# Batch 1's attention outputs with queries on partitions, turned by TensorE, and placed ahead of chunk 24

## The chip, the cores and the metric

The kernel runs on one core of one Trainium2 chip. The metric is the device time of one execution in microseconds (us). Seven executions of the kernel before took 259.46 to 267.28 us, with a median of 260.74 us; the profiled one is the one that took 259.46 us.

## What is computed

The reference is a windowed attention with sink tokens, followed by a gated feed-forward network (ReGLU). It has 4 batches, 8 heads, 768 positions and a head dimension of 64; the network has d_model = 512 and d_ff = 1536.

```
scores = (q @ k.T) / sqrt(64)
keep   = (key < 4) | ((0 <= query - key) & (query - key < 128))
a      = softmax(where(keep, scores, -1e9))
x      = (a @ v), heads side by side: 3072 tokens x 512
out    = (relu(x @ w_gate) * (x @ w_val)) @ w_out
```

The inputs are float32. The kernel computes with bfloat16 operands and float32 sums.

## The kernel before, in words

**Units.** Two heads of one batch make a unit; there are four units to a batch and sixteen in all, `U[4b + p]`. Their 64 head dimensions each fill the 128 partitions.

**Attention of a unit.** `load_kq` or `load_half` brings q and k, a cast on GpSimd makes them bfloat16, and they are turned so that the head dimension lies on partitions. Batch 0 is turned in halves (`T_half`, L292), batch 1 in whole units (`T`, L277), both by TensorE through PSUM; batches 2 and 3 go through DRAM with a transposing DMA (`turn`). ScalarE and VectorE copy the turned keys and queries to `KQ`, where a second copy of the keys at odd offsets is made (`odd_tiles`, L199). `Sg(u, s)` (L316) computes one of three groups of scores, keys on partitions and queries along the free dimension, takes the exponential on ScalarE (L330) and multiplies with a mask on VectorE (L337).

**Outputs of a unit.** There are two ways. `V(u, part)` (L372) multiplies a half of the queries with a block of ones for the sums and with v for the outputs; these come out with the head dimension on partitions, as `xT` needs it, and VectorE turns, inverts and multiplies the sums (L359 to L369). The other way is `W(u)` (L384): queries on partitions, v and a column of ones side by side, so that the sums come with the outputs, then a reciprocal and one multiplication on VectorE. Its result `xn` still has to be turned; the kernel before does this with DMAs through DRAM (`x_to_dram`, `x_turn`). The kernel before takes `V` for batches 0 and 1 and `W` for batches 2 and 3.

**Feed-forward.** `chunk(b, g, m)` (L401) makes one block of 128 hidden columns for half a batch (384 tokens): four matmuls with `wg` (L408), Relu on ScalarE to `gs` (L411), four matmuls with `wv` (L413), and their product on VectorE to `hT` (L415). `ffn2(b, t, m)` (L419 on; matmul L428) adds one of twelve parts of the output of 128 tokens; after the twelfth, ScalarE copies the sum to `ot` (L432) and SP stores it.

**Order.** It is written out by hand, and every engine follows the order in which its instructions are issued. After a head with the first half of batch 0, there are 96 slots, one for each chunk: slot s has chunk s, so that chunk 24 is the first of batch 1. `prep[s]` holds what is issued ahead of the chunk (loads, casts, DMAs), `plan[s]` what follows it: T and H are turns, S scores, V and W outputs, with the unit and the group or half in digits ("S14" is group 4 of unit 1 of the batch). From slot 24 on, three `ffn2` matmuls close each slot; what is left of them at the end makes a tail. Chunk 24 needs the `xT` of all units of batch 1, for the first half of their queries, and chunk 36 for the second.

**Queues and buffers.** Loads and stores are issued by SP in program order, and weights by GpSimd (`load_w`, `load_wo`), which also does the casts of k, q and v in its own order. `gate(u)` (L151) is a small ScalarE copy into a load's buffer; the load waits for it, so it starts no earlier than ScalarE comes to that place. There are three k and q buffers, so unit 7's load needs the buffer that unit 4's cast has read. PSUM has four single banks `G` and two double ones `PP`. Chunks rotate through G[0] to G[2]; G[3] is for `ffn2` and the half turns; scores, outputs and whole turns take the next double bank (`pair`, L261). `wo` comes in three transfers of 512 KB, each for four of the twelve m.

Of the kernel before, what the change touches and what calls it, by code (L numbers as in the profile page):

```python
# [19 lines left out]
def kernel(  # L20
# [12 lines left out]
    nc = tc.nc  # L33
# [60 lines left out]
           5: (0, 0, 499, [(0, 0, 0, 247), (ODD, 120, 247, 499)])}  # L94

    VLAST = [(4, 2, 0, 252, 112), (6, 2, 252, 272, 364), (5, 2, 272, 416, 240), (4, 2, 416, 419, 364)]
    VSEG = [[(0, 0, 8, 252, 0), (1, 0, 252, 504, 120), (0, 0, 504, 507, 244), (2, 1, 0, 140, 244), (3, 1, 252, 264, 372)],
            [(2, 1, 140, 252, 0), (3, 1, 264, 504, 0), (2, 1, 504, 507, 112)] + VLAST]
    VSEG0 = [[(0, 0, 0, 247, 0), (1, 0, 247, 499, 120), (2, 1, 0, 140, 244), (3, 1, 140, 152, 372)],
             [(2, 1, 152, 267, 0), (3, 1, 267, 507, 0)] + VLAST]  # L100


    QSEG = [[(0, 0, 0)], [(0, 0, 128), (1, 0, 252)], [(1, 0, 376), (2, 1, 0), (0, 0, 504)],
# [47 lines left out]
    def gate(u):  # L151

        nc.scalar.copy(kf[u.i % NQ][0:1, 0:2], warm[0:1, :])
# [45 lines left out]
    def odd_tiles(u, copy):  # L199
        e = kE[u.i % NT]  # L200
        copy(odd(e)[:, :, 4:128], e[:, 120:876].rearrange("d (i c) -> d i c", c=252)[:, :, 0:124])
        sinks(u, copy)
# [62 lines left out]
    def two():  # L265
        if head[0]:
            srot[0] += 2
            return G[srot[0] % 4][:], G[(srot[0] + 1) % 4][:]
        x = pair()
        return x[:, 0, :], x[:, 1, :]  # L270
# [5 lines left out]

    def T(u):  # L277
        t = u.i % NT
        tk, tq = two()
        for x, ps in ((kn[u.i % 2], tk), (qn[u.i % 2], tq)):  # L280
            for n in range(NR):
                for h in range(2):
                    r = slice(64 * h, 64 * h + 64)
                    nc.tensor.transpose(ps.bitcast(BF16)[r, 64 * n:64 * n + 64], x[r, 64 * n:64 * n + 64], ident[r, r])  # L284
        vk, vq = (ps.bitcast(BF16)[:, 0:S].rearrange("d (n p) -> d p n", p=PR) for ps in (tk, tq))
        e = kE[t]
        to = lambda ap: ap.rearrange("d (p n) -> d p n", n=NR)
        nc.scalar.copy(to(e[:, 0:S]), vk)
        nc.vector.tensor_copy(to(qT[t]), vq)
        odd_tiles(u, nc.scalar.copy)  # L290

    def T_half(c):  # L292
        t, x = c % NP, c // NP
# [45 lines left out]
    ready = {}  # L339

    def sums(u, part, out, w):
        segs = (VSEG if u.b else VSEG0)[part]
        for i, (j, g, c0, c1, o0) in enumerate(segs):
            for h in range(2):
                nc.tensor.matmul(out=out[64 * h:64 * h + 64, o0:o0 + c1 - c0], lhsT=w(j, h),  # L345
                                 rhs=ee[u.i % NE][:, g, h, c0:c1], start=i == 0, stop=i == len(segs) - 1,
                                 skip_group_check=True)
# [36 lines left out]
    def W(u):  # L384

        ps = pair()
        for h in range(2):
            for t, segs in enumerate(QSEG):
                for i, (j, g, c0) in enumerate(segs):
                    nc.tensor.matmul(out=ps[:, h, 65 * t:65 * t + 65], lhsT=ee[u.i % NE][:, g, h, c0:c0 + 128],  # L390
                                     rhs=vn[u.b % 2][:, j, 2 * u.p + h, 0:65], start=t == 0 and i == 0,
                                     stop=t == 6 and i == len(segs) - 1, skip_group_check=True)
        o = ps[:, :, 0:455].rearrange("p h (t e) -> p h t e", e=65)
        x, r = xn[u.i % 2], rn[u.i % 2]
        nc.vector.reciprocal(r[:], o[:, :, :, 64])
        nc.vector.tensor_tensor(x[:].rearrange("p t (h d) -> p h t d", h=2), o[:, :, :, 0:64],  # L396
                                r[:].unsqueeze(3).to_broadcast([128, 2, 7, 64]), op=Alu.mult)

    gvn = [0]

# [21 lines left out]
    def ffn2(b, t, m):  # L422
        if m == 0:
            ops = OP[tail[0]]
            opn[0] += 1
            opend[b, t] = ops[opn[0] % len(ops)]
        op = opend[b, t]
        nc.tensor.matmul(out=op, lhsT=hT[b % 2][:, m, t * 128:(t + 1) * 128], rhs=wo[:, m, :],  # L428
                         start=m == 0, stop=m == FM - 1)
        if m == FM - 1:  # L430
            ot = outpool.tile([128, d_model], F32, name="ot")
            nc.scalar.copy(ot[:], op)  # L432
            nc.sync.dma_start(out=out[b * S + t * 128:b * S + (t + 1) * 128, :], in_=ot[:])

    with tc.manual_schedule():
# [65 lines left out]
        def put(s, y, n):  # L501
            st = (y[0], n * NP + int(y[1]), int(y[2]) if len(y) > 2 else 0)
            at[st] = s
            plan[s].append(st)

        for s, w in {0: "S04 S02 H1", 1: "S14 S12", 2: "H2", 3: "S24 S22 H3", 4: "S34 S32", 5: "V01", 6: "V11",
                     7: "V21", 8: "V31"}.items():
            for y in w.split():
                put(s, y, 0)
        for s, w in {12: "T0", 13: "T1", 14: "S00 S01", 15: "S10 S11", 16: "T2", 17: "S20 S21", 18: "V00",  # L510
                     19: "V10 T3", 20: "V20", 21: "S30 S31", 22: "V30 S02"}.items():
            for y in w.split():
                put(s, y, 1)
        for s, w in {24: "V01 S12", 26: "V11 S22", 28: "V21 S32", 30: "V31"}.items():
            for y in w.split():
                put(s, y, 1)
        for b, sl in ((2, {29: "S00 S01", 31: "S02 S10", 33: "S11 S12", 35: "S20 S21", 36: "W0", 37: "S22 S30",
# [3 lines left out]
            for s, w in sl.items():  # L521
                for y in w.split():
                    put(s, y, b)
        prep = [[] for _ in slots]
        prep[1] += [("half", 6), ("half", 7), ("v", 0, 3), ("v", 0, 4), ("w", 6, 8), ("v", 0, 5), ("v", 0, 6),
                    ("w", 8, 10), ("w", 10, 12)]
        prep[9] += [("setup3",), ("load", 4), ("load", 5), ("load", 6), ("lv", 1)]
        prep[10] += [("kq", 4), ("load", 7), ("kq", 5)]
        prep[13] += [("kq", 6)]
        prep[15] += [("v", 1, j) for j in range(7)]  # L530
        prep[8] += [("setup2", 0)]
        prep[16] += [("kq", 7), ("wo",)]
        for i, ts in ((8, (14, 18, 19, 23)), (9, (15, 20, 21, 25)), (10, (17, 21, 22, 27)), (11, (19, 22, 23, 29)),
                      (12, (30, 33, 35, 37)), (13, (32, 35, 37, 39)), (14, (34, 37, 39, 41)), (15, (36, 39, 41, 46))):
            for t, what in zip(ts, ("rows", "castrows", "td", "turn")):
# [12 lines left out]
        for s, (b, g, m) in enumerate(slots):  # L548
            for x in prep[s]:
                if x[0] == "kq":  # L550
                    cast_kq(U[x[1]])
                elif x[0] == "load":
                    gate(U[x[1]])
                    load_kq(U[x[1]])
                elif x[0] == "half":
                    cast_half(x[1])
                elif x[0] == "w":
                    load_w(*x[1:])
                elif x[0] == "wo":
                    for c in range(3):  # L560
                        load_wo(c)
                elif x[0] == "rows":
                    load_rows(U[x[1]])
                elif x[0] == "castrows":
                    cast_rows(U[x[1]])
                elif x[0] == "td":
                    to_dram(U[x[1]])
                elif x[0] == "setup3":
                    setup3()
                elif x[0] == "setup2":  # L570
                    setup2(x[1])
                elif x[0] == "xd":
                    x_to_dram(U[x[1]])
                elif x[0] == "xturn":
                    x_turn(U[x[1]])
                elif x[0] == "turn":
                    turn(U[x[1]])
                elif x[0] == "sinks":
                    odd_tiles(U[x[1]], nc.gpsimd.tensor_copy)
                elif x[0] == "lv":  # L580
                    for j in x[2:] or range(7):
                        load_v(x[1], j)
                else:
                    cast_v(*x[1:])
            chunk(b, g, m)
            for what, i, x in plan[s]:
                if what == "T":
                    T(U[i])
                elif what == "H":
                    T_half(NP + i)  # L590
                elif what == "S":
                    Sg(U[i], x)
                elif what == "W":
                    W(U[i])
                else:
                    V(U[i], x)
            for _ in range(3):
                if f2:
                    f2.popleft()()
            if s == 23:  # L600
                f2 += [lambda t=t, mm=mm: ffn2(0, t, mm) for t in range(6) for mm in range(FM)]
            if b > 0 and m == FM - 1:
                f2 += [lambda b=b, t=t, mm=mm: ffn2(b, t, mm) for t in range(3 * g, 3 * g + 3) for mm in range(FM)]
        tail[0] = 1
# [37 lines left out]
```

## Time and profile before

| what | value |
|---|---|
| median of seven runs | 260.74 us |
| the profiled execution's own time | 259.46 us |
| its span, first to last instruction | 257.6 us |
| TensorE busy | 243.3 us, 94% |
| VectorE busy | 137.3 us, 53% |
| ScalarE busy | 116.8 us, 45% |
| GpSimd busy | 69.9 us, 27% |
| slot 0, slot 12 and slot 24 begin at | 20.9, 46.9 and 75.7 us |
| tail of `ffn2` begins at | 238.0 us |

The profile is that of one execution. PE stands for TensorE's matmuls and PEld for its weight loads, DVE for VectorE, ACT for ScalarE, POOL for GpSimd and SP for the engine that only issues DMAs here. Matmuls overlap in the records, so a group of four that starts every 0.65 us can show 0.81 us of busy time; the starts tell the pace. The slots' beginnings are the starts of their first L408 matmul. In the timeline a bracket behind a line gives the idle time of the engine ahead of it and what ended that. The slices are the span cut in 40 pieces of 6.44 us, with the busy share in tenths.

### The profile page before, as it was taken

How to read it: one execution, taken by the hardware profiler on the slowest of the kernel's cores; microseconds unless marked ns; L12 is line 12 of the kernel's file. 1: busy time of each engine (PE TensorE's matmuls, PEld its weight loads, DVE VectorE, ACT ScalarE, POOL GpSimd, SP SyncE). 2: the span in 40 equal slices, each digit the busy share in tenths (PEclk: the TensorE clock that was granted, in tenths of full speed). 3: DMA queues.
4: the chain of work that ended last, by engine and by line, in shares of the span. 5: the costliest groups of instructions: out<-in, count | busy, mean ns of one | idle time of the engine just before them, and what ended most of it. 6: DMA issues, size and time to landing. Idle time of an engine off the chain costs nothing.

```text
span 257.6 us, 5698 instructions
## 1 busy us (share of the span) xinstructions
PE 243.3 (94%) x2255; PEld 141.1 (55%) x2255; DVE 137.3 (53%) x265; ACT 116.8 (45%) x220; POOL 69.9 (27%) x118
## 2 busy tenths in 40 slices
PE   7778899999899999999999999999999999999993
PEld 2444566655656555565655556666555555555441
DVE  7586689578987785666624455644232223223000
ACT  3656842597362556645135664522332333332211
POOL 6593770658432440924001520000000000000000
PEclk9999999999999999999999999999999999999999
DMA  7999994999999999798989802363500111101232
GB/s 195 270 260 195 153 162 140 308 187 362 244 265 236 243 199 281 278 220 194 230 207 222 196 6 71 73 99 105 80 23 26 41 43 41 42 3 41 81 122 81
DMA packets 75571, 40.09 MB, mean 156 GB/s; under 512 B 53529, under 2 KB 71449, under 8 KB 75545
## 3 DMA queue, kind: packets, MB, share of 16 engines
q1 hardware_dynamic: 67080, 34.62, 53.1%
q0 software_dynamic: 7920, 4.72, 13.1%
q10 hardware_dynamic: 544, 0.39, 0.5%
q8 instruction: 17, 0.28, 0.5%
q14 instruction: 10, 0.07, 0.1%
HBM read 28.48 MB, written 11.25 MB: 154 GB/s over the span
## 4 chain that ended last, share of the span: by engine, by line
PE 80%; DVE 8%; ACT 7%; issue 3%; POOL 0%; ACTq 0%; DVEq 0%
PE g L408 22%; PE g L413 21%; PE g L428 20%; PE pp L326 5%; PE pp L428 4%; ACT ee L330 4%; PE pp L345 3%; PE pp L390 3%; ACT KQ L310 1%; DVE KQ L311 1%; PE pp L284 1%; ACT ot L432 1%; DVE R L361 1%; DVE ee L337 1%; PE g L345 1%
## 5 line engine op out<-in xcount | busy, mean ns | idle before, releaser
L415 DVE TENSOR_TENSOR hT<-gs,g 128x384 bf16<-128x384 f32 x96 | 52.9, 551 | 71.4 <-PE g L413 70.1
L411 ACT ACTIVATE gs<-g 128x384 f32<-128x384 f32 x96 | 47.4, 494 | 82.6 <-PE g L408 81.0
L408 PE MATMUL g<-xT,wg 128*128 128x384 bf16 x384 | 78.4, 326 | 0.9 <-DVE hT L415 0.7
L413 PE MATMUL g<-xT,wv 128*128 128x384 bf16 x384 | 78.1, 326 | 0.0
L428 PE MATMUL g<-wo,hT 128*128 128x512 bf16 x240 | 64.0, 380 | 0.2
L408 PEld LDWEIGHTS <-wg 128*128 128x128 bf16 x384 | 36.0, 98 | 32.2 <-issue 1.4
L330 ACT ACTIVATE ee<-pp 128x998 bf16<-128x998 f32 (+4 forms) x52 | 44.4, 901 | 19.1 <-PE pp L326 19.0
L413 PEld LDWEIGHTS <-wv 128*128 128x128 bf16 x384 | 37.5, 98 | 25.0 <-issue 0.2
L428 PEld LDWEIGHTS <-hT 128*128 128x128 bf16 x288 | 26.3, 98 | 25.3 <-issue 0.9
L337 DVE TENSOR_TENSOR ee<-ee,msk 128x838 bf16<-128x838 bf16 (+3 forms) x44 | 31.8, 726 | 13.9 <-ACT ee L330 13.4
L145 POOL CAST vn<-vf 128x512 bf16<-128x512 f32 x28 | 18.1, 653 | 37.7 <-DMA vf<-in_v_dram 36.5
L326 PE MATMUL pp<-KQ 64*128 64x3 bf16 (+7 forms) x320 | 16.6, 223 | 4.6 <-DVE KQ L311 2.8
L432 ACT COPY ot<-g 128x512 f32<-128x512 f32 x20 | 11.7, 587 | 16.1 <-PE g L428 16.1
L326 PEld LDWEIGHTS <-KQ 64*128 64x128 bf16 x320 | 11.2, 94 | 13.9 <-issue 10.5
L182 POOL CAST qn<-qf 128x768 bf16<-128x768 f32 x8 | 7.0, 874 | 24.3 <-DMA kqd<-qn 17.6
L428 PE MATMUL pp<-wo,hT 128*128 128x512 bf16 x48 | 10.7, 379 | 0.0
L345 PEld LDWEIGHTS <-ones 128*64 128x64 bf16 x176 | 7.0, 110 | 5.4 <-issue 4.8
L361 DVE STREAM_TRANSPOSE R<-r 128x384 f32<-128x384 f32 x16 | 9.3, 579 | 0.6
L390 PEld LDWEIGHTS <-ee 128*128 128x128 bf16 x256 | 8.8, 97 | 1.0
L390 PE MATMUL pp<-vn,ee 128*128 128x65 bf16 x256 | 9.0, 193 | 0.0
L396 DVE TENSOR_TENSOR xn<-pp,rn 128x896 bf16<-128x896 f32 x8 | 8.7, 1092 | 0.3
L359 DVE STREAM_TRANSPOSE R<-pp 128x384 f32<-128x384 f32 x12 | 6.9, 577 | 1.2 <-PE pp L345 1.2
(84 smaller groups left out, 152.5 us busy)
## 6 DMA issues: line engine op xcount, KB each, us to landing
out_dram<-ot SPq DMA_DIRECT2D x24, 256.0 KB
kf<-in_k_dram SPq DMA_DIRECT2D x12, 384.0 KB
qf<-in_q_dram SPq DMA_DIRECT2D x12, 384.0 KB
vf<-in_v_dram SPq DMA_DIRECT2D x12, 256.0 KB
vf<-in_v_dram SPq DMA_DIRECT2D x12, 224.0 KB
kf<-in_k_dram SPq DMA_DIRECT2D x8, 192.0 KB
wg<-in_moe_w_gate_dram POOLq DMA_DIRECT2D x6, 256.0 KB, 6.6
wv<-in_moe_w_val_dram POOLq DMA_DIRECT2D x6, 256.0 KB, 7.6
```

Of the source, the lines that this page charges most:

```text
L145: copy(vn[b % 2][0:rows, j, :, 0:64], vf[0:rows, j, :, :])
L326: nc.tensor.matmul(out=ps[:, h, c0:c1], lhsT=kE[t][64 * h:64 * h + 64, x0:x0 + 128], rhs=qT[t][64 * h:64 * h + 64, q0:q0 + c1 - c0], start ...
L330: nc.scalar.activation(x, ps[:, :, b0:n], Act.Exp, bias=0.0, scale=scale)
L337: nc.vector.tensor_tensor(x, x, m.unsqueeze(1).to_broadcast([128, 2, c1 - c0]), op=Alu.mult)
L345: nc.tensor.matmul(out=out[64 * h:64 * h + 64, o0:o0 + c1 - c0], lhsT=w(j, h), rhs=ee[u.i % NE][:, g, h, c0:c1], start=i == 0, stop=i == l ...
L390: nc.tensor.matmul(out=ps[:, h, 65 * t:65 * t + 65], lhsT=ee[u.i % NE][:, g, h, c0:c0 + 128], rhs=vn[u.b % 2][:, j, 2 * u.p + h, 0:65], st ...
L408: nc.tensor.matmul(out=gp[:, 0:CUT], lhsT=wg[:, ko, m * 128:(m + 1) * 128], rhs=x[:, ko, c], start=ko == 0, stop=ko == KO - 1)
L411: nc.scalar.activation(gs[:], gp[:, 0:CUT], Act.Relu, bias=0.0, scale=1.0)
L413: nc.tensor.matmul(out=vp[:, 0:CUT], lhsT=wv[:, ko, m * 128:(m + 1) * 128], rhs=x[:, ko, c], start=ko == 0, stop=ko == KO - 1)
L415: nc.vector.tensor_tensor(h[:, m, c], gs[:], vp[:, 0:CUT], op=Alu.mult)
L428: nc.tensor.matmul(out=op, lhsT=hT[b % 2][:, m, t * 128:(t + 1) * 128], rhs=wo[:, m, :], start=m == 0, stop=m == FM - 1)
L432: nc.scalar.copy(ot[:], op)
```

## The change

Batch 1 takes `W` for its outputs, as batches 2 and 3 do, and a new function `X(u)` turns the result with seven TensorE transposes and one ScalarE copy. All of batch 1's scores and outputs stand ahead of chunk 24. In slot 23, twelve `ffn2` matmuls of batch 0 stand between X2 and X3, and six more after X3; slots 24 and on have three each as before. The segments of `V` for batch 1 are gone (`VSEG` is now what `VSEG0` was).

The half turns H1 to H3 of batch 0 move so that each stands a slot ahead of the scores which read it, and its scores and outputs are spread over slots 0 to 9. In `T`, the turned keys go to G[3] and the queries to a double bank, and the odd-tile copies go to VectorE. The loads of batch 1 move by a slot or two, v of batch 1 comes behind unit 7's k and q in SP's queue, unit 7's load has no `gate` of its own, and unit 7's casts stand ahead of the casts of v on GpSimd. In slot 1's preparation, one pair of weight loads stands ahead of the v casts.

```diff
@@ in T(u)
-        tk, tq = two()
+        tk, tq = G[3][:], pair()[:, 0, :]
...
-        odd_tiles(u, nc.scalar.copy)
+        odd_tiles(u, nc.vector.tensor_copy)
@@ new, after W(u)
+    def X(u):
+        ps = (G[3][:] if u.p < 2 else pair()[:, 0, :]).bitcast(BF16)
+        c = 0
+        for t in range(7):
+            nc.tensor.transpose(ps[:, c:c + 128], xn[u.i % 2][:, t, :], ident[:])
+            c += 128 - t % 2 * 4
+        nc.scalar.copy(xT[u.b % 2][:, u.p, :], ps[:, 8:8 + S])
+        for x in range(2):
+            ready[u.b, u.p, x] = True
@@ plan
-        for s, w in {0: "S04 S02 H1", 1: "S14 S12", 2: "H2", 3: "S24 S22 H3", 4: "S34 S32", 5: "V01", 6: "V11",
-                     7: "V21", 8: "V31"}.items():
+        for s, w in {0: "H1 S04 S02", 1: "H2 S14", 2: "H3 S12", 3: "S24 S22", 4: "S34 S32", 6: "V01", 7: "V11",
+                     8: "V21", 9: "V31"}.items():
...
-        for s, w in {12: "T0", 13: "T1", 14: "S00 S01", 15: "S10 S11", 16: "T2", 17: "S20 S21", 18: "V00",
-                     19: "V10 T3", 20: "V20", 21: "S30 S31", 22: "V30 S02"}.items():
+        for s, w in {12: "T0", 13: "T1", 14: "S00 S01", 15: "S02 S10", 16: "T2 S11", 17: "S12 T3", 18: "W0 S20",
+                     19: "S21 S22", 20: "W1 S30 X0", 21: "S31 S32", 22: "W2 X1", 23: "W3 X2 F X3"}.items():
...
-        for s, w in {24: "V01 S12", 26: "V11 S22", 28: "V21 S32", 30: "V31"}.items():
-            for y in w.split():
-                put(s, y, 1)
+        plan[23].append(("F", 6, 0))
@@ prep
-        prep[1] += [("half", 6), ("half", 7), ("v", 0, 3), ("v", 0, 4), ("w", 6, 8), ("v", 0, 5), ("v", 0, 6),
-                    ("w", 8, 10), ("w", 10, 12)]
-        prep[9] += [("setup3",), ("load", 4), ("load", 5), ("load", 6), ("lv", 1)]
-        prep[10] += [("kq", 4), ("load", 7), ("kq", 5)]
+        prep[1] += [("half", 6), ("half", 7), ("w", 6, 8), ("v", 0, 3), ("v", 0, 4), ("w", 8, 10), ("v", 0, 5),
+                    ("v", 0, 6), ("w", 10, 12)]
+        prep[8] += [("setup2", 0)]
+        prep[9] += [("setup3",)]
+        prep[10] += [("load", 4), ("load", 5), ("load", 6)]
+        prep[11] += [("kq", 4), ("load", 7), ("lv", 1)]
+        prep[12] += [("kq", 5)]
         prep[13] += [("kq", 6)]
+        prep[14] += [("kq", 7)]
         prep[15] += [("v", 1, j) for j in range(7)]
-        prep[8] += [("setup2", 0)]
-        prep[16] += [("kq", 7), ("wo",)]
+        prep[16] += [("wo",)]
@@ the slots
                 elif x[0] == "load":
-                    gate(U[x[1]])
+                    if x[1] < 7:
+                        gate(U[x[1]])
                     load_kq(U[x[1]])
...
+            if s == 23:
+                f2 += [lambda t=t, mm=mm: ffn2(0, t, mm) for t in range(6) for mm in range(FM)]
             for what, i, x in plan[s]:
-                if what == "T":
+                if what == "F":
+                    for _ in range(i):
+                        f2.popleft()()
+                elif what == "X":
+                    X(U[i])
+                elif what == "T":
                     T(U[i])
...
-            for _ in range(3):
+            for _ in range(3 if s > 23 else 0):
                 if f2:
                     f2.popleft()()
-            if s == 23:
-                f2 += [lambda t=t, mm=mm: ffn2(0, t, mm) for t in range(6) for mm in range(FM)]
```

In `plan`, "F" with 12 takes twelve `ffn2` matmuls from the queue; it stands in the string of slot 23, and the six after X3 are appended.

More of the change, by code (lines that the diff above doesn't have):

```diff
@@ L96 @@
     VLAST = [(4, 2, 0, 252, 112), (6, 2, 252, 272, 364), (5, 2, 272, 416, 240), (4, 2, 416, 419, 364)]
[L97 to L100, printed above, removed]
+    VSEG = [[(0, 0, 0, 247, 0), (1, 0, 247, 499, 120), (2, 1, 0, 140, 244), (3, 1, 140, 152, 372)],
+            [(2, 1, 152, 267, 0), (3, 1, 267, 507, 0)] + VLAST]
     QSEG = [[(0, 0, 0)], [(0, 0, 128), (1, 0, 252)], [(1, 0, 376), (2, 1, 0), (0, 0, 504)],
@@ L341, in sums @@
     def sums(u, part, out, w):
-        segs = (VSEG if u.b else VSEG0)[part]
+        segs = VSEG[part]
         for i, (j, g, c0, c1, o0) in enumerate(segs):
@@ L504, in put @@
             plan[s].append(st)
[L506 to L507 removed]
+        for s, w in {0: "H1 S04 S02", 1: "H2 S14", 2: "H3 S12", 3: "S24 S22", 4: "S34 S32", 6: "V01", 7: "V11",
+                     8: "V21", 9: "V31"}.items():
             for y in w.split():
                 put(s, y, 0)
[L510 to L511 removed]
+        for s, w in {12: "T0", 13: "T1", 14: "S00 S01", 15: "S02 S10", 16: "T2 S11", 17: "S12 T3", 18: "W0 S20",
+                     19: "S21 S22", 20: "W1 S30 X0", 21: "S31 S32", 22: "W2 X1", 23: "W3 X2 F X3"}.items():
             for y in w.split():
[L513 to L516 removed]
+                if y == "F":
+                    plan[s].append((y, 12, 0))
+                else:
+                    put(s, y, 1)
+        plan[23].append(("F", 6, 0))
         for b, sl in ((2, {29: "S00 S01", 31: "S02 S10", 33: "S11 S12", 35: "S20 S21", 36: "W0", 37: "S22 S30",
```

## The prediction

> **What bounds the kernel now.** I read the page's busy shares first, then the slices, then TensorE's timeline slot by slot, then the transfers. A slot is one chunk (four L408 and four L413 matmuls) and what follows it.
>
> ```profile
> PE 243.3 (94%) x2255; PEld 141.1 (55%) x2255; DVE 137.3 (53%) x265; ACT 116.8 (45%) x220; POOL 69.9 (27%) x118
> PE   7778899999899999999999999999999999999993
> DMA  7999994999999999798989802363500111101232
> ```
>
> TensorE is the only engine that is nearly full, and the DMA engines are full over the first half. The chain of waits, late in the kernel, shows TensorE with nothing in its way:
>
> ```profile
> 185.62 0.65 PE g L408 x4
> 186.27 0.65 PE g L413 x4
> ```
>
> Four matmuls start in 0.65 us, so a chunk is 1.30 us, and work taken from TensorE there shortens the run one for one. In the slots of batch 0 and 1 (20.9 to 76 us) TensorE's timeline has holes; the bracket is the hole ahead of the line and what ended it:
>
> ```profile
> 25.54 0.53 PE L326 MATMUL pp<-KQ 64*128 64x115 bf16 x12 [0.96 <-DVE KQ L311]
> 32.53 0.53 PE L326 MATMUL pp<-KQ 64*128 64x115 bf16 x12 [0.96 <-DVE KQ L311]
> 45.59 0.81 PE L408 MATMUL g<-xT,wg 128*128 128x384 bf16 x4 [0.70 <-DVE hT L415]
> 59.93 0.63 PE L326 MATMUL pp<-KQ 64*128 64x244 bf16 x12 [0.49 <-ACT gs L411]
> 65.59 0.56 PE L284 MATMUL pp<-ident,kn 64*64 64x64 bf16 x24 [0.67 <-DVE xT L369]
> 71.30 0.40 PE L326 MATMUL pp<-KQ 64*128 64x252 bf16 x6 [0.71 <-DVE xT L369]
> ```
>
> With two more of 0.19 (29.30) and 0.16 (53.40) this is 4.84 us. Last, the output weights `wo`, which the before-kernel first uses at 78.43 us:
>
> ```profile
> 58.64 1.17 POOL L145 CAST vn<-vf 128x512 bf16<-128x512 f32 x2 [0.63 <-DMA vf<-in_v_dram]
> 61.93 2.22 POOL L210 DMA_DIRECT2D wo<-in_moe_w_out_dram  x3
> DMA to landing us min/median/max: 10.8/14.6/18.6
> ```
>
> The three are issued 0.75 us apart from 61.93, so the thirds land at 72.7, 77.3 and 82.0 us. The before-kernel reaches m = 8 (third third) at about 84.1 us: it fits, by two.
>
> **What the skill says.** "TensorE: Matmul & The Clock Gate", Back-to-back issue gap: N/2.4 + 2.5 ns. For 384 columns that is 162.5 ns, and the trace agrees (0.65/4). The same page, Part 1: an idle window of some 3.4 us halves the clock until TensorE has been busy as long; no hole in the slots here is longer than 0.96, so this trace doesn't show it. "DMA: Bandwidth & Descriptors", Queues, rings and completion order: each DMA engine takes turns between the queues that have work. The trace agrees: while SP's queue is full too, `wo` lands a third (512 KB) every 4.7 us, about 110 of 260 GB/s.
>
> **Part by part.** All sums are on the profiled run: span 257.6, its own time 259.46 (1.86 round the span). The median of the seven is 260.74, 1.28 above, so I forecast span + 3.14.
>
> *Half turns ahead (slots 0 to 9).* The holes 0.96, 0.19, 0.96 go: a score no longer meets keys turned in its own slot. What is late next is ScalarE: five gs (0.49), three turned halves (0.81 each with their pieces), four score pairs (1.52): 11 us in slots 0 to 4, against 9.9 us of TensorE. A score then waits for the PSUM pair of the score two before; I take 0.7 (0 to 1.5; it can't fall below 0, as no matmul goes away). So slots 0 to 9 gain 1.4.
>
> *The loads.* They are gated behind chunk 9's gs instead of chunk 8's, but V01 to V31 also start a slot later, so by my count the gate opens at 41.0 us instead of 41.3. Unit 7's load has no gate of its own: the ACT gate that held chunk 10's gs, and so the 0.70 at 45.59, goes. Slot 12 begins at 44.7 instead of 46.9: 2.2 us gained so far. What lies behind unit 7's load in SP's queue pays: all of v of batch 1, by 0.79 MB at 365 GB/s = 2.15 us; SP has a lull at 52 to 54 us (116 GB/s) in that stream that may fill (0 to 1 us back; I take 0.5). Last v cast: 59.8 + 2.15 - 0.3 - 0.5 = about 61.1.
>
> *Slots 12 to 23.* V for a unit takes 0.78 + 0.93 us (61.90 to 62.68, 77.19 to 78.12), W takes 0.96 (109.03 to 109.99), X seven transposes at 0.057 (a half turn's three take 0.17) = 0.40. Four units: 6.84 - 5.44 = 1.4 gained, and four entries into 64-row work of about 0.1, twice, 0.8. Waits behind V20 and V30 of 0.4 in all go. The holes 0.16, 0.49, 0.67, 0.71 (2.03) go; new ones: T1 meets unit 5's queries, which POOL casts until about 49.2, for 0.9 (0 to 1.5), and W0 meets the last v cast for 0.6 (0 to 1.6, by the lull). The second odd-tile copies go to VectorE (502 ns on ScalarE; like-sized VectorE copies 0.22), G[3] lets the two turned halves leave side by side: no TensorE cost. Sum 1.4 + 0.8 + 0.4 + 0.5 = 3.1. The extra mask, W and X copies lie on ScalarE and VectorE beside 28 us of TensorE; each has some 22 us of work there. If that cover fails, what shows is a PSUM wait of about 0.5.
>
> *Later.* S12, S22, S32 and the V?1 leave slots 24 to 30, and 18 `wo` matmuls (0.216 each, 3.9 us) move from the tail into slot 23: moved, not saved. The 0.43 that S20 waits at 106.61 for its odd tiles goes, as that slot comes some 2 us later: 0.4. Turn, out and v transfers of batch 2 stand behind outputs in SP's queue that now start at slot 23; they have 10 us.
>
> Sum without anything new: 2.2 + 3.1 + 0.4 = 5.7, span 251.9, with slot 24 at 79.5.
>
> *The new wait.* In the changed order the fifth and ninth `wo` matmuls of slot 23 wait on the second and third `wo` transfers. These stay behind the v casts on POOL. Casts of unit 7 now stand ahead of v, so the issue is at 61.0 instead of 61.93; the transfers meet the same full SP queue (rows, turned rows), so the third third lands at 81.0 instead of 82.0. By my count slot 23 starts at 72.2: chunk to 73.5, W3 to 74.5, X2 to 74.9, four `wo` matmuls to 75.8, the fifth when the second third lands (77.3 less 1 = 76.3), the eighth done at 77.2. TensorE then stands idle to 81.1, for 3.9 us, and everything (X3, chunk 24 and on) is queued behind. Slot 24 starts at 81.1 + 0.86 (four) + 0.7 (ot copy; X3 in it) + 1.3 (six more) = 84.0, instead of 79.5. Hence 4.5 us of the 5.7 are lost again: span 257.6 - 1.2 = 256.4. I take 256.3 with rounding, run 259.4. Everything in slots 12 to 22 has about 4 us of slack to this landing, so my guesses there hardly count. Bounds of the landing: 79.5 (SP's queue runs dry for a while) to 83 (v lull not filled, issue at 62).
>
> **Rivals.**
> 1. `wo` lands in time, by 77 us or so: no wait, 5.7 us gained, 255.0. For: with no other queue at work the last four gate and value weight transfers (256 KB) landed 1.3 to 1.8 us apart, at 35.2 to 39.6 us. Against: DMA is at 9 in every slice from 45 to 95 us.
> 2. Slower: the third `wo` transfer lands later than now. Place: POOL's queue behind the v casts, and the DMA share. The price is 1 us per us; from 82.2 us on the change loses. SP's queue has fewer waits of its own (castrows 9 no longer waits 0.91 for T3), so it could crowd `wo` more; at 85 to 86 us, with the half clock after an idle stretch of 3.9 us (3.4 us at half, +1.7), the span is 259 to 262: 262 to 265, I say 263.5.
> 3. The order isn't what it says: excluded for TensorE, whose changed order has all W and X ahead of chunk 24. But the holes could only move (T1, W0 and ScalarE in slots 0 to 4 taking all): even with 2 us more of them slot 23's first `wo` matmul comes by 77, and the landing decides again: 259.4.
>
> **How the numbers follow.** Landing decides (with rival 3): 55%, own range 257.9 to 261.6 (landing 79.5 to 83, the half clock at its top). In time: 22%. Slower: 23%. The range 255.3 to 263.5 leaves out about a tenth on each side. About 1% is what a measurement of this kernel can tell from no change: faster by over 1% is under 258.1, slower is over 263.3. Faster: the in-time case and a twentieth of the first, 0.26; slower: the later half of rival 2 and a little of the half clock, 0.18; same 0.56.
>
> **What would show it.** Right: no hole of 0.96 in slots 0 to 4; slot 12 near 44.7; last v cast near 61; slot 23's `wo` matmuls with a hole of about 4 us released by the `wo` transfer; chunk 24 near 84; a tail of 54 matmuls. Wrong: `wo` landing before 78 or after 84, a VectorE or ScalarE hole of over 1 us in slots 14 to 22, or a lower granted clock after slot 23.

## The result and the profile after

The changed kernel is slower. Its median is 264.71 us (260.83 to 267.58, 27 executions) against 260.66 us (259.11 to 267.28, 64 executions) of the kernel before; the ratio is 1.010, with an interval of 1.0077 to 1.0124. The forecast was 259.4 us, with a range of 255.3 to 263.5. The profiled execution took 266.24 us with a span of 264.5. Executions of one kernel differ in their mean TensorE clock (for the changed kernel 260.83 us at full clock, 267.58 at 0.974), so the ratios in this document leave out those over 1.5% above the fastest of their kernel; the profiled one is among these, and its sum below comes out above the ratio.

The page of the changed kernel, busy shares, slices and two groups (busy time and mean ns, then the idle time ahead of the group and what ended most of it); what were L408, L413 and L428 are now L417, L422 and L437:

```profile
PE 245.8 (93%) x2219; PEld 141.5 (53%) x2219; DVE 130.7 (49%) x249; ACT 117.1 (44%) x215; POOL 72.6 (27%) x118
...
PE   7779998998985999999996999999999999999894
...
PEclk9999999999996899999999799999999999999999
DMA  7999975999999898489985971134311111100122
...
L417 PE MATMUL g<-xT,wg 128*128 128x384 bf16 x384 | 78.9, 327 | 3.3 <-DMA xT<-xd 2.4
L437 PE MATMUL g<-wo,hT 128*128 128x512 bf16 x264 | 72.1, 390 | 4.8 <-DMA wo<-in_moe_w_out_dram 3.9
```

TensorE is still the only full engine. Two dents show in its slices, the 13th (79 to 86 us) and the 22nd (139 to 145 us), and with each the granted clock falls, there or in the slice after it. The groups name their causes: 3.9 us of waiting for `wo` and 2.4 us for `xT`. The first was forecast, the second was not.

TensorE's timeline of the changed kernel, first the lines that answer to the holes of before and then slot 23 whole:

```profile
24.96 0.33 PE L324 MATMUL pp<-KQ 64*128 64x115 bf16 x4
...
31.36 0.53 PE L324 MATMUL pp<-KQ 64*128 64x115 bf16 x12
...
45.69 0.81 PE L417 MATMUL g<-xT,wg 128*128 128x384 bf16 x4 [0.67 <-DVE hT L424]
...
62.24 0.22 PE L388 MATMUL pp<-vn,ee 128*128 128x65 bf16 x2 [0.84 <-POOL vn L143]
...
76.34 1.03 PE L437 MATMUL g<-wo,hT 128*128 128x512 bf16 x4
77.55 1.02 PE L437 MATMUL g<-wo,hT 128*128 128x512 bf16 x4 [0.19 <-DMA wo<-in_moe_w_out_dram]
82.24 1.87 PE L437 MATMUL g<-wo,hT 128*128 128x512 bf16 x4 [3.66 <-DMA wo<-in_moe_w_out_dram]
83.90 0.95 PE L402 MATMUL pp<-ident,xn 128*128 128x128 bf16 x7
84.78 2.72 PE L437 MATMUL g<-wo,hT 128*128 128x512 bf16 x6
87.29 0.93 PE L417 MATMUL g<-xT,wg 128*128 128x384 bf16 x4
```

The two holes of 0.96 are gone. The one of 0.70 at chunk 11 is not: it has moved a slot on, with the outputs of batch 0, and stands ahead of chunk 12 (0.67). Slot 12 begins at 45.69 us instead of 46.89, slot 24 at 87.29 instead of 75.68. The forecast hole is there, 3.66 us ahead of the ninth `wo` matmul. What follows it was not in the forecast's middle: four matmuls take 1.87 us where the four at 76.34 took 1.03, because the clock is at half for 6.83 us from 80.7 us on, hole and matmuls together.

GpSimd's timeline of the changed kernel and the summary of the `wo` transfers, which give the landing:

```profile
61.55 1.20 POOL L143 CAST vn<-vf 128x512 bf16<-128x512 f32 x2 [1.41 <-DMA vf<-in_v_dram]
62.70 2.23 POOL L208 DMA_DIRECT2D wo<-in_moe_w_out_dram  x3
```

```profile
DMA to landing us min/median/max: 10.1/14.1/18.0
```

The issue comes at 62.70 us, behind the last v cast, so the third third, issued at 64.16, lands at 82.19 us. TensorE's timeline at chunk 48, the first chunk of batch 2:

```profile
142.56 0.49 PE L417 MATMUL g<-xT,wg 128*128 128x384 bf16 x2
143.97 0.32 PE L417 MATMUL g<-xT,wg 128*128 128x384 bf16 x1 [0.93 <-DMA xT<-xd]
145.79 0.48 PE L417 MATMUL g<-xT,wg 128*128 128x384 bf16 x1 [1.49 <-DMA xT<-xd]
146.06 1.49 PE L422 MATMUL g<-xT,wv 128*128 128x384 bf16 x4
```

Chunk 48 has two of its four `wg` matmuls and waits for the turned outputs of unit 10 and then of unit 11; again the clock is at half behind it, for 3.41 us from 145.5. In the kernel before, it ran without a wait:

```profile
136.50 0.81 PE L408 MATMUL g<-xT,wg 128*128 128x384 bf16 x4
```

The last of its transfers landed at 136.55 us there, and the last of these four matmuls, which needs it, starts about 0.49 us behind the first: there was less than half a microsecond of slack. Beyond chunk 48 TensorE goes from chunk to chunk as before, four matmuls in 0.65 us.

So the way from the forecast span of 256.3 to 264.5 is: the hole ends 1.1 us later (82.24 instead of 81.1); the rest of slot 23 takes 5.05 us instead of 2.9, 2.15 more, at half clock; 2.42 of waiting at chunk 48; about 1.7 for half of the 3.41 us behind it; and 0.67 in the tail at 250.14, where a `wo` matmul waits for the copy of `ot`. These are 8.0 of 8.2 us of this one execution.

### The profile page after: what moved, and what is told of

The parts are those of the page before. It is cut to its first block, busy times and chain, and to the rows that moved or that the text cites. A ratio compares the mean times of both kernels' runs of the same rounds, so it can differ in the third digit from the quotient of the medians.

```text
span 264.5 us, 5607 instructions
## 1 busy us (share of the span) xinstructions
PE 245.8 (93%) x2219; PEld 141.5 (53%) x2219; DVE 130.7 (49%) x249; ACT 117.1 (44%) x215; POOL 72.6 (27%) x118
## 4 chain that ended last, share of the span: by engine, by line
PE 65%; DMA 21%; DVE 4%; ACT 3%; issue 2%; SPq 2%; POOL 2%; ACTq 0%; POOLq 0%
PE g L437 21%; PE g L422 17%; PE g L417 17%; DMA wo<-in_moe_w_out_dram 7%; DMA vf<-in_v_dram 5%; DMA wv<-in_moe_w_val_dram 5%; PE pp L324 3%; PE pp L388 3%; PE pp L437 2%; DMA xd<-xn 2%; ACT ee L328 2%; DMA qf<-in_q_dram 1%; DMA xT<-xd 1%; ACT ot L441 1%; SPq L164 1%
## 5 line engine op out<-in xcount | busy, mean ns | idle before, releaser
L417 PE MATMUL g<-xT,wg 128*128 128x384 bf16 x384 | 78.9, 327 | 3.3 <-DMA xT<-xd 2.4
L422 PE MATMUL g<-xT,wv 128*128 128x384 bf16 x384 | 78.8, 328 | 0.3 <-DMA wv<-in_moe_w_val_dram 0.3
L437 PE MATMUL g<-wo,hT 128*128 128x512 bf16 x264 | 72.1, 390 | 4.8 <-DMA wo<-in_moe_w_out_dram 3.9
L417 PEld LDWEIGHTS <-wg 128*128 128x128 bf16 x384 | 36.1, 98 | 33.9 <-issue 3.1
L422 PEld LDWEIGHTS <-wv 128*128 128x128 bf16 x384 | 37.7, 98 | 27.4 <-issue 2.2
L437 PEld LDWEIGHTS <-hT 128*128 128x128 bf16 x288 | 27.0, 99 | 31.2 <-issue 8.2
L143 POOL CAST vn<-vf 128x512 bf16<-128x512 f32 x28 | 19.2, 696 | 43.0 <-DMA vf<-in_v_dram 43.0
L441 ACT COPY ot<-g 128x512 f32<-128x512 f32 x22 | 12.9, 587 | 26.5 <-PE g L437 26.5
L324 PE MATMUL pp<-KQ 64*128 64x252 bf16 (+7 forms) x320 | 16.8, 227 | 1.1 <-DVE KQ L309 0.9
L388 PE MATMUL pp<-vn,ee 128*128 128x65 bf16 x384 | 13.9, 193 | 1.2 <-POOL vn L143 1.2
L388 PEld LDWEIGHTS <-ee 128*128 128x128 bf16 x384 | 13.3, 97 | 2.9 <-issue 1.4
L394 DVE TENSOR_TENSOR xn<-pp,rn 128x896 bf16<-128x896 f32 x12 | 13.1, 1091 | 0.4
L180 POOL CAST kn<-kf 128x768 bf16<-128x768 f32 x8 | 8.8, 1099 | 1.1 <-DMA kf<-in_k_dram 0.6
L199 POOL COPY KQ<-KQ 128x372 bf16<-128x372 bf16 x8 | 5.6, 696 | 5.2 <-DMA KQ<-kqd 5.2
L273 PE MATMUL g<-idle 128*128 128x512 bf16 x15 | 5.2, 495 | 1.3 <-DVE warm L212 1.3
L147 POOL CAST kn<-kf 128x768 bf16<-128x768 f32 x4 | 3.3, 826 | 8.8 <-DMA kf<-in_k_dram 7.4
```

The costliest lines, as they stand in the source:

```text
L143: copy(vn[b % 2][0:rows, j, :, 0:64], vf[0:rows, j, :, :])
L180: nc.gpsimd.tensor_copy(dst[u.i % 2][:].rearrange("p (n h d) -> p h n d", n=6, h=2), src[u.i % NQ][:].rearrange("p (h n d) -> p h n d", n= ...
L324: nc.tensor.matmul(out=ps[:, h, c0:c1], lhsT=kE[t][64 * h:64 * h + 64, x0:x0 + 128], rhs=qT[t][64 * h:64 * h + 64, q0:q0 + c1 - c0], start ...
L417: nc.tensor.matmul(out=gp[:, 0:CUT], lhsT=wg[:, ko, m * 128:(m + 1) * 128], rhs=x[:, ko, c], start=ko == 0, stop=ko == KO - 1)
L422: nc.tensor.matmul(out=vp[:, 0:CUT], lhsT=wv[:, ko, m * 128:(m + 1) * 128], rhs=x[:, ko, c], start=ko == 0, stop=ko == KO - 1)
```

## The experiments

Unless an edit says otherwise, it is made to the changed kernel. In what follows A is the theory that `wo` and the half clock behind its hole set slot 23, A' that the order in SP's queue sets chunk 48.

**1. Filling the wait.** Sixteen matmuls on a block that nothing reads stand between the eighth and the ninth `wo` matmul of slot 23. They compute nothing that is used; they only keep TensorE busy.

```diff
-                    for _ in range(i):
+                    for j in range(i):
+                        if i == 12 and j == 8:
+                            spin(16, (gvn[0] + 2) % 3)
                         f2.popleft()()
```

> Sixteen idle matmuls (3.5 us of work whose result nobody reads) stand in slot 23 between the eighth and the ninth wo matmul, where the changed kernel's TensorE stood idle for 3.66 us. Theory A (the half clock after the wait is a consequence of the idle time): the clock stays full to chunk 48, chunk 24 begins at about 85.1 us instead of 87.3, and the span falls by about 2.2, to 262.3. Rival C (the half clock is a condition of the chip and has nothing to do with this wait): the clock halves at 80 to 87 us again and chunk 24 stays at 87 or later. The wait of chunk 48 for turned outputs should stay in both, 2.4 us.

TensorE's timeline in slot 23 and at chunk 48 of this version:

```profile
77.05 1.89 PE L437 MATMUL g<-wo,hT 128*128 128x512 bf16 x8
78.77 3.62 PE L273 MATMUL g<-idle 128*128 128x512 bf16 x16
82.22 1.03 PE L437 MATMUL g<-wo,hT 128*128 128x512 bf16 x4
...
143.76 0.32 PE L417 MATMUL g<-xT,wg 128*128 128x384 bf16 x1 [2.90 <-DMA xT<-xd]
145.32 0.48 PE L417 MATMUL g<-xT,wg 128*128 128x384 bf16 x1 [1.24 <-DMA xT<-xd]
```

The last third of `wo` lands at 81.17 us here, while the sixteen are still at work, so the ninth `wo` matmul starts when it did before (82.22 us, 82.24 in the changed kernel). The idle time is gone, and the clock stays full until 144 us: the four matmuls take 1.03 us, and slot 24 begins at 85.22 instead of 87.29. The half clock was thus a consequence of the idle time and cost 2.1 us. But the span is 265.3: chunk 48 comes 2.2 us earlier (140.37), its transfers land only 0.2 to 0.5 us earlier, the wait there grows to 4.14 us, and a half clock of 6.83 us follows. Median 265.19, ratio 1.012 (1.0004 to 1.0236). What is gained in slot 23 is lost again at chunk 48, whose time TensorE doesn't set; the expectation had left the wait there at 2.4 us.

**2. Without the six matmuls behind X3.**

```diff
-        plan[23].append(("F", 6, 0))
```

> The six wo matmuls after X3 in slot 23 are left to the later slots, so the outputs are completed in the same slots as in the kernel before, and each store stands in SP's queue where it stood before; the twelve ahead of X3 stay, and with them the wait for wo. Theory A (chunk 48 waits because the stores now stand ahead of the DMAs of batch 2's turned outputs): the wait of 2.4 us at chunk 48 and the half clock after it go, about 4 us, and the wait for wo stays at 3.7: span about 260. Rival B (chunk 48 is late because the chain of DMAs behind W is slower at its new time, whatever stands where in the queue): the wait stays at 2 us or more, span about 264.

The hole for `wo` is 2.78 us (the last third lands at 80.93 us) with one half-clock stretch of 3.4 us. The wait at chunk 48 shrinks to 0.41 us, with no half clock behind it, and the span is 258.1. Ratio 0.9999 (0.9954 to 1.0044). Leaving out the six moves no work off TensorE, as they come back in the tail; it moves the places at which an output tile is complete and stored. In the changed kernel one store (135.81 us) was issued directly ahead of unit 10's output in SP's queue; here it comes behind unit 10's and 11's. That fits A', but chunk 24 also came 3.9 us earlier, with only one window at half clock, so the two causes aren't parted by this run.

**3. Unit 14's and 15's turns later.** Only the order in the queues changes: unit 14's write (`td`) comes behind the output of unit 10, and its turn (`turn`) and all of unit 15's behind the outputs of both unit 10 and unit 11.

```diff
-    (14, (34, 37, 39, 41)), (15, (36, 39, 41, 46))):
+    (14, (34, 37, 42, 45)), (15, (36, 42, 45, 47))):
```

> The DMAs of unit 14's (and 15's) keys and queries are put behind those of batch 2's outputs in SP's queue (slots 42 and 45 instead of 39 and 41); all else is the changed kernel. Theory A': the turned outputs of units 10 and 11 land some 3 us earlier, chunk 48 doesn't wait, the half clock after it goes, and the span falls by about 4 us to 260.4. Rival B (the transfers of the outputs are slow by themselves): the wait stays at about 2 us. The wait for wo in slot 23 and the half clock there stay in both.

Chunk 48 has no wait any more:

```profile
141.93 0.81 PE L417 MATMUL g<-xT,wg 128*128 128x384 bf16 x4
```

Its last transfer lands at 140.71 us, and the clock is at half only once, for 3.4 us behind the hole for `wo` (3.35). Median 261.27 (20 executions), ratio 0.9943 (0.991 to 0.9976), that is 1.6% below the changed kernel's ratio. A' holds: the turned outputs were late because of what stood ahead of them in SP's queue. That queue in the changed kernel (start, length, operation):

```profile
132.08 2.58 SPq L189 DMA_TRANSPOSE KQ<-kqd  x1
134.75 0.53 SPq L185 DMA_DIRECT2D kqd<-qn  x1
135.34 0.42 SPq L185 DMA_DIRECT2D kqd<-kn  x1
135.81 0.44 SPq L442 DMA_DIRECT2D out_dram<-ot  x1
136.35 2.91 SPq L164 DMA_DIRECT2D xd<-xn  x4
141.06 3.22 SPq L168 DMA_TRANSPOSE xT<-xd  x2
```

W of unit 10 runs at 128.29 us, but its output (`xd`) is written from 136.35 on: unit 14's turn, unit 15's two writes and a store are ahead of it. In the kernel before, with W of unit 10 at 122.24 us, the same part of the queue was:

```profile
125.32 1.34 SPq L191 DMA_TRANSPOSE KQ<-kqd  x1
126.71 0.57 SPq L187 DMA_DIRECT2D kqd<-qn  x1
127.33 0.43 SPq L187 DMA_DIRECT2D kqd<-kn  x1
127.86 2.79 SPq L166 DMA_DIRECT2D xd<-xn  x4
130.75 1.09 SPq L433 DMA_DIRECT2D out_dram<-ot  x1
132.07 2.95 SPq L170 DMA_TRANSPOSE xT<-xd  x2
```

Unit 14's turn and unit 15's writes were ahead of the outputs there too. What is new is that the turn took 2.58 us to issue instead of 1.34 and that the store has come in front; so the write of the outputs is 8.5 us later where W is 6. Why the turn took longer wasn't tried.

**4. Four matmuls and four instead of twelve and six.** Slots 24 and 25 have none, so that the third `wo` transfer isn't needed in slot 23.

```diff
-                    plan[s].append((y, 12, 0))
+                    plan[s].append((y, 4, 0))
...
-        plan[23].append(("F", 6, 0))
+        plan[23].append(("F", 4, 0))
...
-            for _ in range(3 if s > 23 else 0):
+            for _ in range(3 if s > 25 else 0):
```

> In slot 23 four wo matmuls stand ahead of X3 and four after it, and slots 24 and 25 have none, so nothing needs the last third of wo before slot 26. Theory A: no wait over 1 us in slot 23, full clock, chunk 24 at about 79, no wait at chunk 48 as the stores stand nearly where they stood before: span about 253.5, 4 us less than before. Rival R1 (the work itself, W and X on TensorE and the copies on ScalarE, costs what is lost): chunk 24 comes no earlier than 83 and the span is 258 or more.

Slot 24 begins at 80.37 with no wait for `wo`, but the run took 281.02 us (ratio 1.0657, 1.0497 to 1.0818). The experiment failed by its design: with eight matmuls placed ahead and six left out, the twelve of an output end inside a slot's three, and the next output's first matmul then waits for ScalarE's copy out of the only bank:

```profile
98.35 0.78 PE L437 MATMUL g<-wo,hT 128*128 128x512 bf16 x2 [1.81 <-ACT ot L441]
98.93 1.48 PE L417 MATMUL g<-xT,wg 128*128 128x384 bf16 x4
```

Each hole of 1.81 or 1.93 us is followed by 3.41 us at half clock (from 98.6, 112.3, 125.9 and 180.5 us), those of 0.67 by none. So it settles nothing on A or A'.

**5 and 6. Three and three, alone and with the turns of run 3.** Six matmuls in all, which is what slots 24 and 25 had, keep the twelve in step with the slots.

```diff
-                    plan[s].append((y, 12, 0))
+                    plan[s].append((y, 3, 0))
...
-        plan[23].append(("F", 6, 0))
+        plan[23].append(("F", 3, 0))
...
-            for _ in range(3 if s > 23 else 0):
+            for _ in range(3 if s > 25 else 0):
```

> The changed kernel, with three wo matmuls ahead of X3 and three after it, and none in slots 24 and 25: six are done by slot 25 as in the kernel before, outputs are completed in the same slots as before, always at the end of a slot, and m = 8 comes in slot 26. Theory A (the loss is the wait for wo with its half clock, and the stores' places in SP's queue with the wait of chunk 48): chunk 24 at about 78.5 us, no hole over 1 us in slot 23 and at chunk 48, full clock, span about 253.9, run about 255.8, 1.8% below before. Rival R1 (W, X and the copies cost what they save): span 257 or more.

> As the run before it, and unit 14's and 15's DMAs behind those of the outputs as in the earlier run. If chunk 48 is on the edge of its turned outputs (0.41 us late in the run without the six), this gives up to 0.5 us more: span about 253.5. If it isn't, the same as the run before it.

Slot 24 begins at 78.03 and 78.16 us, as A has it, yet the spans are 257.0 and 257.6; ratios 0.9977 (0.9947 to 1.0007) and 0.9924 (0.989 to 0.9957). With the turns later the 1.14 us that chunk 48 still waited in run 5 is gone. But both runs have a new hole in slot 35, at the scores of unit 10. TensorE's line of run 6, and GpSimd's timeline ahead of it:

```profile
105.00 0.53 PE L324 MATMUL pp<-KQ 64*128 64x252 bf16 x10 [2.82 <-POOL KQ L195]
```

```profile
101.94 0.83 POOL L180 CAST qn<-qf 128x768 bf16<-128x768 f32 x1 [4.28 <-DMA qf<-in_q_dram]
102.97 0.83 POOL L180 CAST kn<-kf 128x768 bf16<-128x768 f32 x1 [0.20 <-DMA kf<-in_k_dram]
...
104.30 0.50 POOL L199 COPY KQ<-KQ 128x372 bf16<-128x372 bf16 x1
```

Unit 10's turned keys landed at 96.13 us. Their odd-tile copy (104.30) stands on GpSimd behind the casts of unit 12's rows, and GpSimd sat 4.28 us waiting for those to land. In run 6 the clock is at half for 3.41 us from 106.2 us, behind this hole. The kernel before had this wait too: it is the 0.43 us at 106.61, which the prediction saw but read as a matter of the slot's time. Of the versions that bring slot 35 forward with batch 1's new order, each runs into it (runs 5, 6 and 8) until run 9 changes GpSimd's order; runs 7 and 10, where slot 35 comes only 1.1 us earlier than before, don't.

**7. The half turns alone**, in the kernel before.

```diff
-        for s, w in {0: "S04 S02 H1", 1: "S14 S12", 2: "H2", 3: "S24 S22 H3", 4: "S34 S32", 5: "V01", 6: "V11",
-                     7: "V21", 8: "V31"}.items():
+        for s, w in {0: "H1 S04 S02", 1: "H2 S14", 2: "H3 S12", 3: "S24 S22", 4: "S34 S32", 6: "V01", 7: "V11",
+                     8: "V21", 9: "V31"}.items():
```

> The kernel before, with only the order of half turns, scores and outputs of batch 0 in slots 0 to 9 taken from the changed kernel. The prediction's step: 1.4 us gained in slots 0 to 9, slot 12 at about 45.5 and the span at about 256.2. Rival: slots 12 to 22 wait for batch 1's keys, queries and v, which come no earlier, and the gain is given back: span 257 to 257.6.

Slot 12 begins at 45.07 us instead of 46.89, so 1.8 us are gained, and 1.7 of them last until chunk 48 (134.80 instead of 136.50). There TensorE waits 0.60 and 0.98 us for `xT`, whose last transfer lands at 137.15 us, and the span is 257.8 against 257.6. Ratio 0.998 (0.9953 to 1.0006). The gain is real and is given back at chunk 48, in the kernel before just as in the changed one.

**8. V of unit 3 a slot later**, on top of run 6, for the hole ahead of chunk 12.

```diff
-        ... 8: "V21", 9: "V31"}.items():
+        ... 8: "V21", 10: "V31"}.items():
```

> As the second run of this call, with V31 in slot 10 instead of 9. The hole of 0.67 us ahead of chunk 11, which the prediction put down to the gate on ScalarE, is still there without that gate. Theory D: VectorE is behind, with 2.5 us of work to a slot of 2.28 in slots 6 to 9 (hT, two turns, reciprocal, product), and the free slot lets it catch up: the hole goes and slot 12 begins 0.67 earlier; the span gains up to 0.67 unless batch 1's loads set the end of it. Rival: the hole stays and ScalarE or a bank of PSUM ends it.

The hole, which the expectation still puts at chunk 11, falls from 0.67 to 0.27 us: it was VectorE, which in run 6 has no gap from 38 to 45 us, with the units' sums to turn, invert and multiply; what is left waits for VectorE's `xT` of unit 3. The run as a whole settles nothing: a wait of 0.79 us for `wv` at 22.39 us hides the gain by slot 12 (45.26; 44.97 in run 6), and the hole in slot 35 is longer, 3.52 us (median 261.04, ratio 0.9971, 0.9925 to 1.0017).

**9. The casts of unit 12's rows behind the odd-tile copies** (and unit 13's a slot later), on top of run 6.

```diff
-    (12, (30, 33, 35, 37)), (13, (32, 35, 37, 39)),
+    (12, (30, 35, 36, 38)), (13, (32, 36, 38, 40)),
```

> As the version with three and three wo matmuls and unit 14's and 15's turns later, and the row casts of unit 12 on GpSimd at slot 35 instead of 33, of unit 13 at 36 instead of 35 (their writes and turns one or two slots later). Theory: the 2.82 us hole ahead of the scores of unit 10 (slot 35, at 102.2) is the odd-tile copy of unit 10, whose turned keys landed at 96.1 and which stands on GpSimd behind unit 12's row casts, whose loads land at 101.9 and 102.9. With the casts behind the copies the hole is under 0.5 and no half clock follows it: slot 36 at about 102.2 instead of 106.1, chunk 48 at about 132 without a wait for xT, last matmul 249, span 253.1, run 255.0. Rival (SP's queue gives it back): the hole goes, but chunk 48 then waits for the xT of units 10 and 11 for 2 us or more; span 255 to 257.5. Rival (the turned keys themselves): the hole stays.

GpSimd's timeline of this version, then TensorE's in slot 35:

```profile
98.62 0.95 POOL L199 COPY KQ<-KQ 128x372 bf16<-128x372 bf16 x1
99.52 0.55 POOL L195 COPY KQ<-KQ 128x12 bf16<-128x12 bf16 x1
102.03 0.83 POOL L180 CAST qn<-qf 128x768 bf16<-128x768 f32 x1 [1.96 <-DMA qf<-in_q_dram]
```

```profile
101.19 0.63 PE L324 MATMUL pp<-KQ 64*128 64x244 bf16 x12
```

The copy is done at 100.07 us, some 1.1 us before the scores start, slot 36 begins at 102.41 instead of 106.11, no half clock is left, and chunk 48 begins at 131.19 with its last transfer landed at 130.92. Median 254.67 us (254.03 to 255.39), ratio 0.9752 (0.9712 to 0.9792), 2.5% faster than the kernel before and the best of all versions. The rival, that chunk 48 would give it back, failed, though by 0.3 us only.

**10. The half turns and the turns of run 3**, in the kernel before: run 7 with the edit of run 3.

> The kernel before with the half turns a slot ahead and, besides, unit 14's and 15's turned writes and turns later in SP's queue. Theory: the 1.7 us that the half turns gained until slot 48 were lost there because the xT of units 10 and 11 stand in SP's queue behind unit 14's write and turn; with these behind them chunk 48 starts at 134.8 without a wait (1.58 before), last matmul at 252.0, span 256.2. Rival (the xT transfers land by their own chain from W's outputs, whatever is ahead in the queue): holes of 0.60 and 0.98 stay, span 257.8.

SP's queue of this version, with the line numbers of the kernel before, to be held against the one shown at run 3:

```profile
123.05 0.84 SPq L166 DMA_DIRECT2D xd<-xn  x2
123.99 0.86 SPq L187 DMA_DIRECT2D kqd<-qn  x1
...
128.22 2.69 SPq L170 DMA_TRANSPOSE xT<-xd  x2
131.01 1.41 SPq L191 DMA_TRANSPOSE KQ<-kqd  x1
```

The transfers to `xT` now come ahead of unit 14's turn and land by 132.47 us, chunk 48 begins at 134.75 without a wait, and the span is 255.8. Median 258.26, ratio 0.9904 (0.9865 to 0.9943). So the order in SP's queue is what had taken the half turns' gain. Run 9 is 3.5 us of span ahead of this one. That is what W and X, the other new turns and loads, the `wo` matmuls of slot 23 and the free slot 35 give together; no run parts them.

**11. `wo` issued ahead of the v casts**, in slot 14 behind unit 7's casts.

```diff
-        prep[14] += [("kq", 7)]
+        prep[14] += [("kq", 7), ("wo",)]
...
-        prep[16] += [("wo",)]
```

> The changed kernel with the three wo transfers issued on GpSimd behind unit 7's casts (slot 14), ahead of the v casts. Theory A (wo is late because GpSimd comes to its issue late, behind the v casts): issue at 55.4 instead of 62.7, thirds land at about 61, 66 and 71, no wait for wo in slot 23. The v of batch 1 shares the DMA engines with wo: W0 waits about 3 us more than its 1.18 (v cast last at about 65.5); slot 24 at 83 to 84 instead of 87.3; a half clock after W0's wait is possible. Rival (DMA share: the last third needs until 79 or later wherever it is issued, because the rows and turned rows are moved at the same time): a hole for wo of over 1 us stays in slot 23.

The thirds land at 61.40, 65.34 and 68.77 us and nothing waits for `wo`: the place on GpSimd is what made it late. But the v transfers behind it stop. GpSimd's and TensorE's timelines:

```profile
65.92 0.62 POOL L143 CAST vn<-vf 128x512 bf16<-128x512 f32 x1 [7.05 <-DMA vf<-in_v_dram]
```

```profile
66.59 0.33 PE L388 MATMUL pp<-vn,ee 128*128 128x65 bf16 x3 [5.54 <-POOL vn L143]
70.40 0.27 PE L388 MATMUL pp<-vn,ee 128*128 128x65 bf16 x2 [3.48 <-POOL vn L143]
```

W0 waits 9.3 us where about 4.2 were expected, with 10.24 us at half clock around it, and slot 24 begins at 91.25. Median 268.47, ratio 1.0292 (1.0232 to 1.0352). The expectation's theory is right on the cause and was wrong on the price: with 1.5 MB of `wo` in the middle of the v stream, the last wait of a v cast for its tile ends at 69.73 us instead of 61.55, 8.2 us later.

## Why the prediction was wrong

Point by point, by its own steps.

- *Half turns ahead*: right in kind, and too low in size. Slots 0 to 11 took 24.66 us instead of 25.98, with 0.35 of waiting for `wv` in them that the moved weight loads brought (30.60 us), and with the hole of VectorE still there, ahead of chunk 12. Run 7 gave 1.8. The 0.7 us set aside for ScalarE didn't appear.
- *The loads*, "the ACT gate that held chunk 10's gs, and so the 0.70 at 45.59, goes": wrong. The gate went and the hole stayed, released by VectorE's `hT`. The before-trace named VectorE and the step overruled it; run 8 confirmed VectorE. With the 0.35 above this is about the 1.0 us by which slot 12 is later than forecast.
- *Slots 12 to 23*: right in sum. From slot 12 to the last chunk of batch 1's preparation (slot 23) the forecast was 27.5 us and 28.0 were measured. No wait shows at T1 (0.9 forecast), and 1.18 at W0 (0.6 forecast) since the last v cast came 1.6 us later than put.
- *The new wait*: right in mechanism and place, down to the matmul; the landing was mis-sized by 1.2 us, as the issue came at 62.70 and not at 61.0. By the forecast's own rule 82.2 was the point from which the change loses, and it landed at 82.19. This step alone thus gives a change of nothing; what made the kernel slower is in the next two.
- *The half clock* was kept at the top of the range, on the reading of the Trainium skill's "TensorE: Matmul & The Clock Gate" (Part 1), that it takes an idle window of some 3.4 us. The forecast hole of 3.9 us was longer than that, so by this reading itself the half clock belonged on the likeliest path, which priced it at nothing. It cost 2.1 us (run 1 against the changed kernel). The runs show it behind shorter holes as well: 1.81 (run 4) and, in two pieces, 0.93 and 1.49 at chunk 48.
- *Later*, "turn, out and v transfers of batch 2 stand behind outputs in SP's queue [...] they have 10 us": this is the step that failed most. The turned outputs of units 10 and 11 had not 10 us but less than half a microsecond of slack at chunk 48 in the kernel before (landed 136.55, chunk begun at 136.50, its last `wg` matmul needing unit 11). In the changed kernel W of these units and chunk 48 come some 6 us later, but their last transfer lands 9.2 us later, behind unit 14's slower turn and the store; that is 2.42 us of wait and about 1.7 of half clock. Runs 3 and 10 show the queue's order as the cause by changing that order and no work; the 1.7 is an estimate, half of the 3.41 us of the stretch.
- *S20's 0.43 goes*: right for the changed kernel, where slot 35 came 6.9 us later and not 2, but what the wait hung on, the casts ahead of the copy on GpSimd, wasn't read. Where slot 35 came earlier than before, the same wait was 2.5 to 3.5 us (runs 5, 6, 8). Rival 1, `wo` in time at 255.0, would have failed on this and on chunk 48: run 5, in which nothing waits for `wo`, has 257.0 of span where that rival had 251.9.

Of the rivals, the second (slower, `wo` later and a half clock behind it) has the first 3.3 us of the miss; the larger rest lay in no case. The sum itself is borne out as a whole. With the `wo` matmuls, SP's order and GpSimd's order set right (run 9) the span is 252.3 us, against the 251.9 of "sum without anything new", and the holes that are left are small ones (0.67, 0.94 and 0.43, all three ended by VectorE). That its parts are right one by one isn't shown: the half turns gave more than forecast, and the 0.67 stayed.

## What to carry to other kernels

Before a stage is moved, look for the transfers that land just when they are needed, not only for holes: a landing within half a microsecond of its use (here 136.55 us, for a chunk begun at 136.50) took back the whole gain ahead of it in run 7. Then read what stands ahead of that transfer in its in-order queue, on SP as on GpSimd, and ask of each entry what it waits for; here two moves of entries that were needed later took 1.6% (run 3 against the changed kernel) and 1.7% (run 9 against run 6), with no work taken away. And price a hole of about 2 us or more with the half clock that can follow it, not by its length alone (2.1 us here, run 1).

## What was not expected of the hardware

- The half clock came in stretches of 3.41 us or multiples (6.83 and 10.24), also behind single holes of 1.81 to 1.93 us (four of four in run 4) and of 2.78 us (run 2). The length of a hole doesn't decide alone: in run 5 one of 2.46 us had none behind it, and in run 4 one of 1.14 us had a stretch begin 2 us later. The Trainium skill's "TensorE: Matmul & The Clock Gate" (Part 1) speaks of an idle window of about 3.4 us; its length agrees with the stretches, but as a bound for holes it is too high here.
- Where the hole falls counts. Within a trace the stretches begin whole multiples of 3.41 us apart: in run 4 at 64.5, 98.6, 112.3, 125.9 and 180.5 us, which are 10, 4, 4 and 16 steps, and in the changed kernel at 80.7 and 145.5 us, 19 steps. Cut into these steps, the 2.46 us of run 5 are 0.95 in one and 1.51 in the next, while the two holes at chunk 48 of the changed kernel lie in one step (2.17 us idle in all). Over all thirteen traces, from slot 0 to the last matmuls, each of the twelve steps that had full clock and 1.8 us or more of idle time was followed by half clock; of five with 1.44 to 1.75 us one was (that of run 4, with 1.48), and of those with less none.
- Two queues don't share evenly whatever is in them. The Trainium skill's "DMA: Bandwidth & Descriptors" (Queues, rings and completion order) has each DMA engine take turns between queues that have work, by packets. With rows and turned rows in SP's queue `wo` landed a third every 4.7 us in the changed kernel, which is 110 of the 268 to 289 GB/s moved in that time; with the v tiles in it (run 11) a third every 3.4 to 3.9 us, 133 of 195 and 153 of 247 GB/s, and a v tile issued at 54.20 us, 0.03 us after the first third, landed only at 65.87 us, 4.5 us after that third. Why v fares so much worse wasn't tried.
